# State products of heads 2 and 3 put on the other half of the array and into a second PSUM bank, and a new list of attention's order

## The chip, the cores and the metric

The kernel runs on one core of a Trainium2 chip. The metric is device time of one execution in microseconds (us). A core has five engines with a program each: TensorE (PE, with its weight loads shown apart as PEld), VectorE (DVE), ScalarE (ACT), GpSimd (POOL) and SyncE (SP, which here only issues DMAs). Each runs its own instructions in the order in which they were written and waits on semaphores for the others.

## The reference

```python
def _attn_ref(q, k, v, a_re, a_im):            # (4, 8, 768, 48) each
    mag = np.sqrt(a_re * a_re + a_im * a_im)
    scale = np.minimum(mag, 0.999) / (mag + 1e-06)
    a_re_n, a_im_n = (a_re * scale, a_im * scale)
...
    for t in range(S):                          # complex state, 48 x 48 a head
        new_re = ar * S_re - ai * S_im
        new_im = ar * S_im + ai * S_re
        S_re, S_im = (new_re + kv, new_im)
        y[:, :, t] = np.einsum('bhd,bhde->bhe', q[:, :, t], S_re)
...
def _moe_ref(x, w_gate, w1, w2):                # x: (3072, 384), 8 experts, F = 1024
    expert_idx = np.argmax(logits, axis=1)      # each token to one expert
...
        h = np.maximum(xe @ w1[e], 0.0)
        out[mask] = gate_w[mask, None] * (h @ w2[e])
```

## The kernel before

Attention comes first, then the experts. Attention is written in chunks of 128 positions: 4 batches of 6 chunks, 24 in all (chunk 2.3 is the fourth of the third batch). Ten *units* of one, two or three chunks (`UNITS`) go through `front`, elementwise work of ACT and DVE (logarithms, exponentials, scans and sines of the gates). Its last two DVE operations write `cz` and then `Z` of the unit, queries and keys turned by the accumulated phase, real and imaginary part; four small DMAs move the pieces of heads 6 and 7 to `cm`. Units 0 to 9 start at chunks 0.0, 0.1, 0.3, 1.0, 1.3, 2.0, 2.3, 3.0, 3.3 and 3.5.

`chunk` is PE's part. Per chunk there are transposes of the keys (L381, L383), scores into banks 0 and 1 (L394, and L402 for heads 6 and 7), which DVE masks into `am` (two operations), the **state products**, queries times the state that the earlier chunks left (L416, and L422 for heads 6 and 7; 20 chunks have them, a batch's first has none), `am` times values (L432), and, where more chunks follow, the new state (L442, L447). State products and value products accumulate in bank 4 (`YT`). ACT copies it to `yt` (L435), PE turns it (L455, bank 6, `XT`), ACT copies that to `xg` (L458). A float32 matmul shows as two MATMUL records. Heads lie in pairs: an even head on partitions 0 to 47, an odd one on 64 to 111, of the operands and of the result alike, `side(h)`:

```python
for g in range(G):                       # L416: three pairs of heads
    for part in range(2):
        for h in (2 * g, 2 * g + 1):
            nc.tensor.matmul(YT[side(h), g * 128:g * 128 + 128], lhsT=sb[1 - par][side(h), s0:s0 + D], rhs=wide[part][side(h), g, 0], ...)
```

After each batch (in pieces for the last) `route` takes the gate's argmax on DVE, counts places with small matmuls (L496 to L501) and POOL scatters rows to DRAM. When the last chunk is done, `fill` runs 256 tokens of the fullest expert (L616, L624), and then the eight experts follow (L784, L800), PE-bound, in an order that `M` plans by itself.

No engine is scheduled at run time: attention's operations are numbered as the code lists them, and `ORDER`, a list of these numbers in base 36, says in which order they are written. It sets the order on every engine and on SP's DMA queue. The duration that stands first in each `P.add` served the making of such a list; with the list given it does nothing. The first column of bank 7 holds ones (`ones_t`), which DVE's phase scans (L326) read.

Of the kernel before, what the change touches and what calls it, by code (L numbers as in the profile page):

```python
# [14 lines left out]
ACT = mybir.ActivationFunctionType  # L15
# [7 lines left out]
G = 3  # L23
# [5 lines left out]
SWAPPED = (2, 3, 7)  # L29
NZ = 4  # L30
# [26 lines left out]
0 1 1g 3 2 4 5 6 7 8 3e 9 1i 1j a c j b 1k 1h d e 1l l m k f n g 1m 3g i 3h h o 1n 1o p q r  # L57
1y 3i 1p 1r 3j s 1s t 3f 3k 1z 21 v 1q w 1u u 20 22 1t 10 3l 1v 1x 1w 6a 16 y 23 24 25 x 13 3m 3w 3n 3z 3p 27 26
3y z 3o 6c 3q 6d 14 28 3r 11 6e 15 17 3s 12 3x 3t 3u 29 2a 2b 2e 6f 40 6g 19 1c 41 6s 42 18 1a 43 6b 2c 44 2h 1d 2d 1b
3v 8r 45 2i 2j 6h 46 2k 2f 1e 49 6i 47 48 2g 2z 6j 6m 2w 30 8t 6k 6l 4a 2l 2n 2s 8u 2x 4b 31 2m bq 2y 6n 2t 1f 2o 4g 4d  # L60
6o 2p 6p 8v 4h 8w 4e 8x 3a 32 6t 2q 2r 6q 4i 6u bs 33 36 6r 35 6v 34 8y 2u 4j 4k 3b 6w 4f 6x 2v 6y 37 8z 4c 4m 4l 90 bt
6z 8s 38 39 71 4r 4v 4y br bu 51 52 4n 70 91 4o 53 3c 54 93 92 72 78 99 4p 4w 4s 4q 4z 55 5d 56 3d 95 73 bv 50 4x 5e 57
4t 94 74 98 bw 76 75 59 5g 7e 5f 9b 4u 58 77 9a 5b e5 7h bx 9c 7b 7c 5a 7f 96 5c 97 9d 7i by 7d 7g 5h bz 5i 7k 7j 5j 9e
7u c8 5k 9f 7r 7s 7v 7x c1 c0 c2 7y 9g 7t 7l 5l 7n 9h 80 7z 9j 9i e6 7w 8f 89 5m 7o 9k 5n 7m 5o 8g 81 8c c4 5p 7p 5v 8h
5w c3 e7 9p 9m 8a e8 c7 8i 5x 8d 82 5q 9l 83 85 7q 5r 5s 5t c9 9n 9o 8b 5y 5z 8e 9q 9t 9u 9r c5 h8 60 e9 ca c6 86 9s 9w
8n 84 9v cb ea a8 87 eb 9x 9y 5u ec 8j 8k 9z ha ab cd 8o cc 8l 68 65 ce ae 69 ed ee 8m eg 88 af 8p hb a0 ag ah a1 cf a4
# [927 lines left out]
```

## Time and profile before

| what | value |
|---|---|
| median of 3 runs | 494.07 us (489.94 to 500.96) |
| profiled execution | 494.87 us |
| its span, first to last instruction | 493.2 us |
| PE busy | 435.2 us (88%) |
| DVE busy | 245.2 us (50%) |
| ACT busy | 207.1 us (42%) |
| start of `fill`'s first matmul | 220.7 us |

The span is what the profile's rows cover; 1.7 us of the execution lie outside it. A start in the rows is counted from the span's start. Busy shares are means over attention and experts, which have different limits, so the stretches have to be read one by one.

### The profile page before, as it was taken

The page shows a single profiled execution, that of the slowest core. Times are in us where ns is not written, and L with a number is a line of the kernel's source. Part 1 is how long each engine was busy: PE and PEld are TensorE (multiplying, and loading weights), DVE is VectorE, ACT ScalarE, POOL GpSimd, SP SyncE. Part 2 cuts the span into 40 slices and gives each one's busy share as a digit, 9 for nine tenths or more (in the row PEclk, how much of TensorE's full clock was granted, in tenths as well). Part 3 has the DMA queues.
Part 4 walks back from the last instruction along what each step waited for, and adds up shares of the span by engine and source line. Part 5 has one row for each costly group of instructions (what it writes and reads, how often), then busy time and mean ns, then how long its engine had stood idle before and what let it go on. Part 6 is the DMA issues. An engine that isn't in the chain of part 4 may idle for free. (4 is left out here: it accounts for less than half of the span.)

```text
span 493.2 us, 10498 instructions
## 1 busy us (share of the span) xinstructions
PE 435.2 (88%) x4402; PEld 303.3 (62%) x4402; DVE 245.2 (50%) x436; ACT 207.1 (42%) x319; POOL 89.3 (18%) x156
## 2 busy tenths in 40 slices
PE   0134998989898889989999999999999999999995
PEld 0023887878787788977775545555555455655563
DVE  6999999999988877733321131312212012111101
ACT  5999999989979577722001001000000010000000
POOL 8100022053203817022100000100101020010102
PEclk9999999999989998999999999999999999999999
DMA  8347674655948444561999832912504313010001
GB/s 277 117 170 225 197 276 95 229 171 167 247 117 268 113 143 116 135 247 60 282 391 373 208 83 48 282 60 96 130 0 161 105 72 132 16 32 17 28 1 47
DMA packets 31542, 73.11 MB, mean 148 GB/s; under 512 B 19955, under 2 KB 21900, under 8 KB 28160
## 3 DMA queue, kind: packets, MB, share of 16 engines
q1 hardware_dynamic: 28160, 62.49, 42.0%
q0 software_dynamic: 3184, 9.86, 5.3%
q8 instruction: 36, 0.59, 0.5%
q14 instruction: 18, 0.15, 0.1%
q10 hardware_dynamic: 144, 0.03, 0.0%
HBM read 55.65 MB, written 12.29 MB: 138 GB/s over the span
## 5 line engine op out<-in xcount | busy, mean ns | idle before, releaser
L784 PE MATMUL bank<-xrt,w1b 128*128 128x432 f32 (+6 forms) x336 | 114.5, 498 | 0.0
L800 PE MATMUL bank<-w2b,ht 128*128 128x384 f32 x336 | 110.7, 486 | 0.0
L792 ACT ACTIVATE ht<-bank 128x384 f32<-128x384 f32 (+1 forms) x32 | 14.8, 464 | 223.1 <-PE bank L784 223.1
L784 PEld LDWEIGHTS bank<-xrt,w1b 128*128 128x128 f32 x336 | 63.7, 190 | 48.8 <-issue 22.9
L800 PEld LDWEIGHTS bank<-w2b,ht 128*128 128x128 f32 x336 | 63.8, 190 | 44.5 <-issue 1.4
L789 DVE TENSOR_SCALAR ht<-bank 128x384 f32<-128x384 f32 (+1 forms) x32 | 16.8, 524 | 92.0 <-PE bank L784 91.5
L632 POOL DMA_INDIRECT out_dram<-yo,hg x22 | 21.6, 980 | 220.7 <-DVE yo L724 175.0
L724 DVE TENSOR_SCALAR yo<-bank,hg 128x384 f32<-128x384 f32 x22 | 13.6, 618 | 83.6 <-PE bank L800 83.6
L259 ACT ACTIVATE AB<-AB 128x1152 f32<-128x1152 f32 (+5 forms) x46 | 45.5, 998 | 3.8 <-DVE first L572 1.6
L515 POOL DMA_INDIRECT xs_hbm<-xg,slot x24 | 33.4, 1391 | 39.1 <-issue 13.9
L159 POOL TENSOR_TENSOR Z<-Z,C 128x1152 f32<-128x1152 f32 (+2 forms) x7 | 16.0, 2288 | 126.0 <-DMA AB<-in_gates_u_dram 48.2
L381 PE MATMUL bank<-order,cz 128*128 128x128 f32 x60 | 11.4, 305 | 28.3 <-DVE cz L159 22.2
L159 DVE TENSOR_TENSOR am<-bank,mask 128x512 f32<-128x512 f32 x48 | 31.6, 681 | 7.3 <-PE bank L402 3.8
L159 DVE TENSOR_TENSOR Z<-Z,AB 128x1152 f32<-128x1152 f32 (+4 forms) x20 | 31.7, 1589 | 3.5 <-ACT AB L259 3.1
L432 PE MATMUL bank<-am,v 128*48 128x128 f32 x384 | 28.4, 291 | 5.6 <-DVE am L159 5.0
L394 PE MATMUL bank<-Z 48*64 48x64 f32 (+1 forms) x576 | 30.8, 255 | 2.4 <-DVE Z L159 1.2
L394 PE MATMUL bank<-cz 48*64 48x64 f32 (+1 forms) x576 | 29.9, 262 | 0.8 <-DVE am L159 0.4
L682 ACT ACT_TABLE_LOAD x23 | 29.5, 1283 | 1.7 <-PEq L979 1.3
L416 PE MATMUL bank<-cz,sb 48*48 48x128 f32 x240 | 24.9, 275 | 3.1 <-issue 2.0
L432 PEld LDWEIGHTS bank<-am,v 128*48 128x48 f32 x384 | 22.9, 131 | 7.1 <-DVE am L159 5.2
L416 PE MATMUL bank<-Z,sb 48*48 48x128 f32 x240 | 24.7, 270 | 2.4 <-issue 2.4
L394 PEld LDWEIGHTS bank<-Z 48*64 48x64 f32 x576 | 24.1, 141 | 3.2 <-issue 1.6
(166 smaller groups left out, 632.8 us busy)
## 6 DMA issues: line engine op xcount, KB each, us to landing
w2b<-in_w_dram SPq DMA_DIRECT2D x7, 1536.0 KB
w1b<-in_w_dram SPq DMA_DIRECT2D x7, 1536.0 KB
AB<-in_gates_u_dram SPq DMA_DIRECT2D x6, 1152.0 KB
Z<-in_qk_u_dram SPq DMA_DIRECT2D x6, 1152.0 KB
v<-in_v_u_dram SPq DMA_DIRECT2D x8, 792.0 KB
wA<-in_w_dram SPq DMA_DIRECT2D x4, 768.0 KB
xs_hbm<-htA SPq DMA_DIRECT2D x2, 1045.0 KB
xr<-xs_hbm SPq DMA_DIRECT2D x12, 156.0 KB
```

What stands on the lines that cost most here:

```text
L159: return (eng or nc.vector).tensor_tensor(out=o, in0=a, in1=b, op=op)
L259: lambda: nc.scalar.activation(o, i, func=f, scale=scale, bias=bias, **kw), r, w, tag)
L394: nc.tensor.matmul(SC[h % 2][y:y + 64, g * 128 + x:g * 128 + 128], lhsT=wide[part][side(h), g, 1, x:x + 64], rhs=wide[part][side(h), g, 0, ...
L416: nc.tensor.matmul(YT[side(h), g * 128:g * 128 + 128], lhsT=sb[1 - par][side(h), s0:s0 + D], rhs=wide[part][side(h), g, 0], start=(g == 0 ...
L432: nc.tensor.matmul(YT[side(h), (h // 2) * 128:(h // 2) * 128 + 128], lhsT=values(h), rhs=am[2 * par + h % 2][:, h // 2, :], start=(c == 0 ...
L515: i = nc.gpsimd.indirect_dma_start(out=xs_hbm[:, :], out_offset=bass.IndirectOffsetOnAxis(ap=R[slot][:, c:c + 1], axis=0), in_=xg[:, (g0 + ...
L632: i = nc.gpsimd.indirect_dma_start(out=out[:, :], out_offset=bass.IndirectOffsetOnAxis(ap=index, axis=0), in_=y, in_offset=None, bounds_ch ...
L682: nc.scalar.preload_act_table_set("natural_log_exp_and_others" if P.cur == "LE" else "trig_and_small")
L784: nc.tensor.matmul(HB[hb][:, 0:nt], lhsT=a[:, c:c + 128], rhs=xrt[s][:, d, 0:nt], start=(d == 0), stop=(d == DT - 1))
L789: M.add("DVE", 0.00105 * n + 0.12, lambda o=o, k=k, n=n, hb=hb: nc.vector.tensor_scalar_max(o, HB[hb][:, k:k + n], 0.0), (("H", hb),), (ko,))
L792: M.add("ACT", 0.00085 * n + 0.12, lambda o=o, k=k, n=n, hb=hb: nc.scalar.activation(o, HB[hb][:, k:k + n], func=ACT.Relu), (("H", hb),), ...
L800: nc.tensor.matmul(OB[ob][:, 0:DM], lhsT=ht[s][:, f_, j * 128 - k0:j * 128 - k0 + 128], rhs=w[:, f_ * DM:f_ * DM + DM], start=(f_ == 0), s ...
```

## The change

`PLACE` gives each pair of heads its 128 columns of `yt`: pair 0 stays at 0, pair 2 moves to 128, pair 3 to 256, pair 1 (heads 2 and 3) to 384. Heads 2 and 3 write to bank 7 (`YU`), with sides exchanged: head 2 (operands on partitions 0 to 47) to partitions 64 to 111, head 3 to 0 to 47. The loop of the state products has part outside and pairs inside. ACT copies 384 columns of bank 4 and 128 of bank 7, two instructions per chunk for one. The turning matrix and the gate's weights follow the exchanged sides. The ones move to column 511 of bank 7, bank 7 is set to zero at the start, and the scans no longer name bank 7 as an operand of the plan. The whole of `ORDER` is new. The planned duration of a state product goes from 1.345 to 0.95.

```diff
+PLACE = (0, 3, 1, 2)
...
-0 1 1g 3 2 4 5 6 7 8 3e 9 1i 1j a c j b 1k 1h d e 1l l m k f n g 1m 3g i 3h h o 1n 1o p q r
+0 1 1h 3h z 3 2 4 1i 5 6 3i 6h 7 1j 8 1k 9 1l 1m j a b c d k 1n l e f m 1o g 3j i h 3k o n p
...
-    ones_t = bank[7][:, 0:1]
-    nc.vector.memset(ones_t, 1.0)
-    for x in (4, 0, 1):
+    for x in (4, 0, 1, 7):
         nc.vector.memset(bank[x], 0.0)
     nc.vector.memset(bank[5], 0.0)
+    ones_t = bank[7][:, 511:512]
+    nc.vector.memset(ones_t, 1.0)
...
-                    (Bk, ("tend", b, c0), "b7"), (("si", s, g),))
+                    (Bk, ("tend", b, c0)), (("si", s, g),))
...
+            def out(h):
+                g = h // 2
+                o = 64 * (h % 2 != (g == 1))
+                x = 128 * PLACE[g]
+                return YU[o:o + D] if g == 1 else YT[o:o + D, x:x + 128]
...
-                    for g in range(G):
-                        for part in range(2):
+                    for part in range(2):
+                        for g in range(G):
                             for h in (2 * g, 2 * g + 1):
                                 s0 = part * G * D + g * D
-                                nc.tensor.matmul(YT[side(h), g * 128:g * 128 + 128], lhsT=sb[1 - par][side(h), s0:s0 + D],
-                                                 rhs=wide[part][side(h), g, 0], start=(g == 0 and part == 0), stop=False, skip_group_check=True)
-                P.add("PE", 1.345, f, (("sb", 1 - par),) + ZK[0] + ZK[1], (("YT", 0), ("YT", 1)))
+                                nc.tensor.matmul(out(h), lhsT=sb[1 - par][side(h), s0:s0 + D],
+                                                 rhs=wide[part][side(h), g, 0], start=(g < 2 and part == 0), stop=False, skip_group_check=True)
+                P.add("PE", 0.95, f, (("sb", 1 - par),) + ZK[0] + ZK[1], ("YT", "b7"))
...
-            P.add("ACT", act_t(512) - 0.06, lambda: nc.scalar.copy(yt[par], YT), (("YT", 0), ("YT", 1)), (("yt", par),))
+            P.add("ACT", act_t(384) - 0.06, lambda: nc.scalar.copy(yt[par][:, 0:384], YT), ("YT",), (("yt", par),))
+            P.add("ACT", act_t(128) - 0.06, lambda: nc.scalar.copy(yt[par][:, 384:512], YU), ("b7",), (("yu", par),))
...
-                        nc.tensor.matmul(XT[x:x + 64, p * 104:p * 104 + 104], lhsT=yt[par][:, p * 128 + x:p * 128 + x + 64], rhs=turn[:, p, :],
+                        nc.tensor.matmul(XT[x:x + 64, p * 104:p * 104 + 104], lhsT=yt[par][:, PLACE[p] * 128 + x:PLACE[p] * 128 + x + 64], rhs=turn[:, p, :],
```

**PE, the first state products (chunk 0.1).** `sb` is the state, `cz` and `Z` are the two parts, `cm` the pieces of heads 6 and 7, `bank4` and `bank7` the results; x2 is a pair of heads. Before:

```order
L383 MATMUL bank2_63<-order_95,cm1_204 128x112
L416 MATMUL bank4_65<-cz1_201,sb0_216 48x128 x2
L416 MATMUL bank4_65<-Z1_194,sb0_216 48x128 x2
L416 MATMUL bank4_65<-cz1_201,sb0_216 48x128 x2
L416 MATMUL bank4_65<-Z1_194,sb0_216 48x128 x2
L416 MATMUL bank4_65<-cz1_201,sb0_216 48x128 x2
L416 MATMUL bank4_65<-Z1_194,sb0_216 48x128 x2
L381 MATMUL bank3_64<-order_95,Z2_195 128x128 x3
```

And now:

```order
L424 MATMUL bank4_65<-cz1_202,sb0_217 48x128 x2
L424 MATMUL bank7_68<-cz1_202,sb0_217 48x128 x2
L424 MATMUL bank4_65<-cz1_202,sb0_217 48x128 x2
L424 MATMUL bank4_65<-Z1_195,sb0_217 48x128 x2
L424 MATMUL bank7_68<-Z1_195,sb0_217 48x128 x2
L424 MATMUL bank4_65<-Z1_195,sb0_217 48x128 x2
L464 MATMUL bank6_67<-turn_114,yt0_215 64x104 x8
```

The same twelve matmuls follow each other as three pairs of one part and then three of the other, the second pair of each in bank 7.

**DVE, the end of unit 5 (first chunk 2.0).** `cz2` and `Z1` are the unit's results, `am0` and `am1` the masked scores of chunk 1.4, `am2` and `am3` those of chunk 1.5; the rows with `lend` are scans of unit 6, `AB1<-AB1,C1` is a product of unit 7. Before:

```order
L313 TENSOR_SCALAR AB0_190<-AB0_190 128x1152
L315 SCALAR_TENSOR_TENSOR AB0_190<-AB0_190,lend_69,C0_197 128x384
L159 TENSOR_TENSOR am0_208<-bank0_61,mask_100 128x512
L159 TENSOR_TENSOR am1_209<-bank1_62,mask_100 128x512
L315 SCALAR_TENSOR_TENSOR AB0_190<-AB0_190,lend_69,C0_197 128x384 x2
L159 TENSOR_TENSOR AB1_191<-AB1_191,C1_198 128x1152
L159 TENSOR_TENSOR cz2_202<-Z1_194,AB2_192 128x2304
L159 TENSOR_TENSOR Z1_194<-Z1_194,AB2_192 128x2304
L291 COPY lend_69<-AB0_190 128x3x3
L159 TENSOR_TENSOR am3_211<-bank1_62,mask_100 128x512
L159 TENSOR_TENSOR am2_210<-bank0_61,mask_100 128x512
```

And now:

```order
L315 TENSOR_SCALAR AB0_191<-AB0_191 128x1152
L161 TENSOR_TENSOR am2_211<-bank0_61,mask_101 128x512
L317 SCALAR_TENSOR_TENSOR AB0_191<-AB0_191,lend_69,C0_198 128x384
L161 TENSOR_TENSOR cz2_203<-Z1_195,AB2_193 128x2304
L161 TENSOR_TENSOR am1_210<-bank1_62,mask_101 128x512
L161 TENSOR_TENSOR Z1_195<-Z1_195,AB2_193 128x2304
L161 TENSOR_TENSOR am0_209<-bank0_61,mask_101 128x512
L317 SCALAR_TENSOR_TENSOR AB0_191<-AB0_191,lend_69,C0_198 128x384 x2
L161 TENSOR_TENSOR AB1_192<-AB1_192,C1_199 128x1152
L328 SCALAR_TENSOR_TENSOR AB0_191<-bank7_68,tend_71,AB0_191 128x384
L161 TENSOR_TENSOR am2_211<-bank0_61,mask_101 128x512
L293 COPY lend_69<-AB0_191 128x3x3
```

(The first `am2` of the second list is chunk 1.3's.) Two scans, a product and one mask stood ahead of `Z1` and now stand behind it, but chunk 1.5's masks stand further back, with one phase scan more ahead of them.

**ACT, the copies of the first chunk's result (chunk 0.0).** `yt` receives bank 4, and now bank 7 too; rows with `AB` belong to units. Before:

```order
L259 ACTIVATE AB2_192<-AB2_192 128x1152
L259 ACTIVATE AB2_192<-AB2_192,hpi_81 128x1152
L450 COPY sb0_216<-bank5_66 112x384
L435 COPY yt0_214<-bank4_65 128x512
L259 ACTIVATE AB2_192<-AB2_192 128x1152
```

And now:

```order
L444 COPY yt0_215<-bank7_68 128x128
L261 ACTIVATE AB2_193<-AB2_193 128x1152
L459 COPY sb0_217<-bank5_66 112x384
L443 COPY yt0_215<-bank4_65 128x384
L261 ACTIVATE AB2_193<-AB2_193 128x1152
```

One copy became two, here with two other instructions between them.

## Rows read from the trace of the kernel before

**Rows 1.** The page's busy lines, its 40 slices of 12.3 us (tenths of busy time, the granted clock, the DMA share) and its lines on instruction packets.

```profile
PE 435.2 (88%) x4402; PEld 303.3 (62%) x4402; DVE 245.2 (50%) x436; ACT 207.1 (42%) x319; POOL 89.3 (18%) x156
PE   0134998989898889989999999999999999999995
DVE  6999999999988877733321131312212012111101
ACT  5999999989979577722001001000000010000000
q8 instruction: 36, 0.59, 0.5%
q14 instruction: 18, 0.15, 0.1%
```

**Rows 2.** Busy time by stretch: from, to and length in us, then PE, PEld, DVE, ACT, POOL with instruction counts, granted clock, DMA share, GB/s.

```profile
50.00:125.00 75.00, 71.03 (x1536) 61.10 (x1529) 74.17 (x85) 72.84 (x96) 16.46 (x10) 1.00 0.63 190
125.00:207.00 82.00, 72.95 (x1556) 64.39 (x1555) 65.81 (x117) 64.76 (x102) 28.82 (x20) 0.96 0.58 166
221.00:243.00 22.00, 22.00 (x101) 15.94 (x100) 8.06 (x47) 3.46 (x10) 4.13 (x5) 1.00 0.47 135
243.00:489.00 246.00, 244.76 (x818) 141.84 (x816) 45.35 (x99) 16.69 (x52) 23.74 (x25) 1.00 0.37 119
```

**Rows 3.** PE in order of time: start, us to the last end, operation and count. One chunk's state products and what follows.

```profile
120.47 0.42 PE L416 MATMUL bank<-cz,sb 48*48 48x128 f32 x4
120.72 0.39 PE L416 MATMUL bank<-Z,sb 48*48 48x128 f32 x4
120.94 0.39 PE L416 MATMUL bank<-cz,sb 48*48 48x128 f32 x4
...
121.91 0.43 PE L422 MATMUL bank<-cm,sb 112*48 112x128 f32 x4
122.17 1.05 PE L432 MATMUL bank<-am,v 128*48 128x128 f32 x16
123.04 0.88 PE L455 MATMUL bank<-turn,yt 128*64 128x104 f32 x16
```

**Rows 4.** The same view: three transposes on the whole array, and one chunk's scores (48 matmuls of 128 or 64 columns into two banks, from the first row of L394 to L402).

```profile
89.18 0.49 PE L381 MATMUL bank<-order,cz 128*128 128x128 f32 x3
89.51 0.36 PE L383 MATMUL bank<-order,cm 112*128 112x112 f32 x2
89.79 0.44 PE L394 MATMUL bank<-cz 48*64 48x128 f32 x8
...
91.05 0.56 PE L402 MATMUL bank<-cm 112*64 112x128 f32 x8
```

**Rows 5.** The state products alone, by stretch: PE, PEld (instructions), clock, DMA share, GB/s. 24 matmul records are a chunk.

```profile
48.00:125.00 77.00, 13.83 (x216) 11.38 (x216) 1.00 0.63 192
125.00:221.00 96.00, 17.95 (x264) 14.54 (x264) 0.96 0.60 175
148.50:221.00 72.50, 14.09 (x208) 11.16 (x204) 0.98 0.58 173
```

**Rows 6.** ACT's copies by line: count, busy us, mean ns, idle time before them and who ended it.

```profile
L385 ACT COPY kt<-bank 128x384 f32<-128x384 f32 x40 | 17.9, 479 | 1.1 <-PE bank L383 1.0
L435 ACT COPY yt<-bank 128x512 f32<-128x512 f32 x24 | 14.1, 588 | 9.5 <-PE bank L432 9.2
```

**Rows 7.** DVE in order of time around the end of unit 5.

```profile
115.03 1.26 DVE L159 TENSOR_TENSOR am<-bank,mask 128x512 f32<-128x512 f32 x2
116.21 1.92 DVE L315 TENSOR_TENSOR_SCAN AB<-AB,lend,C 128x384 f32<-128x384 f32 x2
118.04 1.33 DVE L159 TENSOR_TENSOR AB<-AB,C 128x1152 f32<-128x1152 f32 x1
119.29 2.55 DVE L159 TENSOR_TENSOR cz<-Z,AB 128x2304 f32<-128x2304 f32 x1
121.95 2.56 DVE L159 TENSOR_TENSOR Z<-Z,AB 128x2304 f32<-128x2304 f32 x1
124.50 1.28 DVE L159 TENSOR_TENSOR am<-bank,mask 128x512 f32<-128x512 f32 x2
125.70 1.01 DVE L326 TENSOR_TENSOR_SCAN AB<-bank,tend,AB 128x384 f32<-128x384 f32 x1
```

**Rows 8.** PE's first work on unit 5 (scores of chunk 2.0), and on unit 6 (scores of chunk 2.3), with the idle time before it.

```profile
125.84 0.44 PE L394 MATMUL bank<-cz 48*64 48x128 f32 x8 [0.39 <-DVE am L159]
148.94 0.32 PE L394 MATMUL bank<-cz 48*64 48x128 f32 x1
```

**Rows 9.** DVE between the ends of units 5 and 6: every row of that stretch with idle time before it, and unit 6's last product.

```profile
141.60 0.33 DVE L471 TENSOR_REDUCE lg<-xg 128x24 f32<-128x96 f32 x1 [0.79 <-ACT xg L458]
142.81 0.69 DVE L159 TENSOR_TENSOR am<-bank,mask 128x512 f32<-128x512 f32 x1 [0.89 <-PE bank L402]
143.42 2.55 DVE L159 TENSOR_TENSOR Z<-Z,AB 128x2304 f32<-128x2304 f32 x1
```

**Rows 10.** PE stopping with "issue" as the reason, in order of time, and a wait for the last batch's counts.

```profile
136.19 0.33 PE L447 MATMUL bank<-v,kt 128*48 128x48 f32 x3 [2.00 <-issue]
158.08 0.31 PE L416 MATMUL bank<-Z,sb 48*48 48x128 f32 x2 [2.12 <-issue]
184.22 0.20 PE L496 MATMUL bank<-oh,before 128*128 128x48 bf16 x1 [1.24 <-ACT C L259]
188.49 0.41 PE L394 MATMUL bank<-Z 48*64 48x128 f32 x3 [0.41 <-issue]
189.23 0.29 PE L394 MATMUL bank<-Z 48*64 48x128 f32 x2 [0.33 <-issue]
189.97 0.34 PE L394 MATMUL bank<-Z 48*64 48x64 f32 x3 [0.45 <-issue]
216.97 0.42 PE L416 MATMUL bank<-cz,sb 48*48 48x128 f32 x4 [1.31 <-issue]
```

**Rows 11.** The view of rows 2, of the first of these stops, of the 3.2 us behind it and of a later stretch.

```profile
133.90:136.30 2.40, 0.40 (x16) 0.28 (x10) 2.33 (x7) 2.38 (x3) 0.00 (x0) 1.00 0.99 352
136.40:139.60 3.20, 3.20 (x24) 2.45 (x22) 3.20 (x4) 2.23 (x4) 0.00 (x0) 0.50 0.57 234
190.90:194.30 3.40, 3.40 (x59) 3.40 (x56) 3.03 (x4) 0.92 (x2) 3.10 (x2) 0.50 0.53 120
```

More of the change, by code (lines that the diff above doesn't have):

```diff
@@ L62 @@
[L62 to L66, printed above, removed]
@@ L80 @@
+n9 nj na ng ot nk nb ou pk nc nh ni nl nn pi nm ov pj l2 po ow pl ox oy oz p5 pm p0 p6 pp p1 p7 pb p2 pc p8 p3 pn p4 pu
+p9 pd pa pe pq pv pf ps pr pg py ph pw q2 px pt pz q3 q0 q1
 """
@@ L241, in gateloop_then_moe @@
         P = Plan()
-        SC, KT, YT, ST, XT, RT = bank[0:2], bank[2:4], bank[4], bank[5], bank[6], bank[6][:, 416:416 + C * E]
+        SC, KT, YT, YU, ST, XT, RT = bank[0:2], bank[2:4], bank[4][:, 0:384], bank[7][:, 0:128], bank[5], bank[6], bank[6][:, 416:416 + C * E]
         def act_t(n):
@@ L411, in f @@
                 def f():
[L412 to L413 removed]
+                    for part in range(2):
+                        for g in range(G):
                             for h in (2 * g, 2 * g + 1):
                                 s0 = part * G * D + g * D
[L416 to L418 removed]
+                                nc.tensor.matmul(out(h), lhsT=sb[1 - par][side(h), s0:s0 + D],
+                                                 rhs=wide[part][side(h), g, 0], start=(g < 2 and part == 0), stop=False, skip_group_check=True)
+                P.add("PE", 0.95, f, (("sb", 1 - par),) + ZK[0] + ZK[1], ("YT", "b7"))
                 def f():
                     for j in range(2):
[L422 removed]
+                        nc.tensor.matmul(out(6 + j), lhsT=sb[1 - par][0:112, 2 * G * D + j * D:2 * G * D + j * D + D],
                                          rhs=last2[:, j, 0], start=False, stop=False, skip_group_check=True)
[L424 removed]
+                P.add("PE", 0.25, f, (("sb", 1 - par), "YT") + MK, ("YT",))
             def values(h):
@@ L431, in f @@
                 for h in range(H):
-                    nc.tensor.matmul(YT[side(h), (h // 2) * 128:(h // 2) * 128 + 128], lhsT=values(h),
-                                     rhs=am[2 * par + h % 2][:, h // 2, :], start=(c == 0 and h < 2), stop=True, skip_group_check=True)
-            P.add("PE", 0.88, f, (("v", i % NV), ("am", 2 * par), ("am", 2 * par + 1), ("YT", 0), ("YT", 1)), (("YT", 0), ("YT", 1)))
-            P.add("ACT", act_t(512) - 0.06, lambda: nc.scalar.copy(yt[par], YT), (("YT", 0), ("YT", 1)), (("yt", par),))
+                    nc.tensor.matmul(out(h), lhsT=values(h),
+                                     rhs=am[2 * par + h % 2][:, h // 2, :], start=(c == 0 and h < 4), stop=True, skip_group_check=True)
+            P.add("PE", 0.88, f, (("v", i % NV), ("am", 2 * par), ("am", 2 * par + 1), "YT", "b7"), ("YT", "b7"))
+            P.add("ACT", act_t(384) - 0.06, lambda: nc.scalar.copy(yt[par][:, 0:384], YT), ("YT",), (("yt", par),))
+            P.add("ACT", act_t(128) - 0.06, lambda: nc.scalar.copy(yt[par][:, 384:512], YU), ("b7",), (("yu", par),))
             if not last:
```

46 lines of the change are left out of this document (24 added, 22 removed).

## The prediction, made before the changed kernel ran

> **What bounds the kernel now.** I read the page's slices first. DVE stands at 9 from the second slice to the twelfth, ACT at 8 or 9 to the eleventh, PE at 8 or 9 from the fifth to the end [rows 1]. So attention has a part where three engines are full at once, and the experts are PE's alone. The view by stretches confirms it: from 50 to 125 us DVE is busy 74.17 of 75 us and ACT 72.84, PE 71.03; from 125 to 207 us PE has 72.95 of 82 us and DVE and ACT some 65 each; from 221 us on PE is busy all but 1.2 us [rows 2]. The first matmul of `fill` follows attention's last value products and nothing in the change touches what comes behind it, so I take the 22 us of `fill` and the 246 us of the experts as a block that moves as a whole. The question is by how much attention ends earlier than 221 us.
>
> Second, the waits. At 125.84 us PE begins the scores of chunk 2.0 after a wait for DVE, and DVE's `Z` of unit 5, which these scores also need, ended at 121.95 + 2.56 = 124.51 us [rows 7, 8]. So until 125 us DVE sets the pace, and what PE saves there is lost in waiting. Unit 6's `Z` ends at 143.42 + 2.55 = 145.97 us [rows 9] and PE takes it up at 148.94 us [rows 8]: from there PE is the late one. In both stretches PE also stops with "issue" as reason: 2.00, 2.12 and 1.31 us are the large ones [rows 10]. During the first, DVE and ACT went on, the DMA share was 0.99, and the clock granted afterwards was 0.50, its 1.2 GHz level, for 3.2 us or so [rows 11]. Instructions come by DMA as well (36 and 18 packets [rows 1]), so packets that wait behind bulk loads are the reading that I give "issue".
>
> **The state products.** Four records (two heads, two records each) of 128 columns start every 0.22 to 0.25 us [rows 3], 55 ns a record at the smaller, while three whole-array transposes of 128 columns take 89.51 - 89.18 = 0.33 us, 110 ns each [rows 4]. So two heads of a pair already run side by side, each at 110 ns, and a chunk costs 12 x 0.11 = 1.32 us. Scores use all four quarters of the array and two banks: 48 records in 91.05 - 89.79 = 1.26 us, 26 ns each [rows 4]. With heads 2 and 3 on the other two quarters and in another bank, pairs 0 and 1 can run together; pairs 0 and 2 share their quarters, so these remain: 2 pairs x 2 parts x 2 records x 0.11 = 0.88 us. That saves 0.44 us a chunk, 8.8 us over 20 chunks. From below the bound is 0 (two at a time stays the limit), from above 0.70 us (26 ns a record as in the scores, 1.32 - 24 x 0.026), though the shared quarters speak against that end. I take 0.44: the scores' row is the same shape of work. The value products keep 16 records, alternating less regularly between halves (left, right, right, left); their 0.87 us [rows 3] stays, at most 0.2 us a chunk more if two heads on one half follow each other badly.
>
> A rule speaks against it. The Trainium skill, TensorEngine Tiling (Array Packing), section Restrictions and Gotchas, says that different row tiles cannot access the same PSUM bank at the same time. The two heads of a pair are on different row tiles and write bank 4, and they overlap all the same [rows 3, 4], on different partitions; by the rule a chunk would take 24 x 0.11 = 2.6 us before. Here the trace disagrees; if the rule came back with four at a time, two would remain and nothing would be saved, which is the second rival below.
>
> **Until 125 us: -1 us.** Nine chunks' state products lie there (216 records [rows 5]); their 4.0 us are covered by DVE, which has 0.8 us free in 75 [rows 2]. ACT gets 24 copies more. 512 columns take 588 ns and 384 take 479 [rows 6], 0.85 ns a column, so 128 should take 479 - 256 x 0.85 = 261 ns and a chunk costs 479 + 261 - 588 = 0.15 us more. Some 10 of the 24 fall where ACT is full: 1.5 us, of which I count 1 as a loss, since ACT has 2.2 us free there. The added memset of bank 7 is one more of DVE's first instructions, when DVE waits for the first loads; it costs nothing, at most 0.5 us. On DVE the end of unit 5 moves forward past two scans, a product and a mask: (118.04 - 116.21) + (119.29 - 118.04) + (116.21 - 115.03)/2 = 3.7 us [rows 7]. But the scores of chunk 2.0 also need the score banks, which the masks of chunk 1.5 free, and those have one phase scan (0.95 us) more ahead of them. So I count nothing for it here.
>
> **From 125 to 149 us: +3 us.** PE's work shrinks by three state products, 1.3 us, and the stop of 2.00 us with the half clock behind it (3.2 us at half rate, 1.6 us of work lost [rows 10, 11]) may go or stay. DVE bounds it: up to unit 6's `Z` the lists hold the same work to within 0.2 us, and DVE idled 0.79 + 0.89 = 1.68 us between the two units' ends [rows 9], so `Z` can come 1.7 us earlier; with the 2.9 us that PE lags (148.94 - 145.97), PE can gain 4.6 us by the scores of chunk 2.3. Between 0 and 4.6 I take 3, nearer to the upper end, since the order now gives PE the masks when it needs them and three shorter products come on top.
>
> **From 149 us on: +3.5 us,** eight state products (208 records [rows 5]) x 0.44, on PE's own path: DVE had 16 us free from 125 to 207 [rows 2] and can follow.
>
> **Packets: +1.5 us.** Behind 149 us PE stopped 2.12 + 0.41 + 0.33 + 0.45 + 1.31 = 4.6 us for issue [rows 10]. The new list moves loads on SP past other work, so these stops move too; no row tells where to. Between -5 (as many again) and +4.6 I take a third of what stands there.
>
> Sum: -1 + 3 + 3.5 + 1.5 = 7.0 us. The profiled execution (494.87 us) is 0.8 us from the median of the runs, so I subtract from the median: 494.07 - 7.0 = **487.1 us**. A measurement of this kernel tells some 2%, 9.9 us, from no change.
>
> **The rivals.** *The stops go as well.* Then 125 to 149 us gives 4.6, the 4.6 us of stops vanish, and so do the half clock of 190.9 to 194.3 us (3.4 us at half rate, 1.7 us [rows 11]) and the 1.24 us wait at 184.22 us [rows 10]: -1 + 4.6 + 3.5 + 4.6 + 1.7 + 1.2 = 14.6, less a third for stops that arise elsewhere, 10 to 14: about 482. For it: DVE had 16 us free. Against: 54 packets must still come through the same loads. *Two at a time stays the limit,* or DVE's masks hold PE: 3.5 falls away, 3 becomes 1.5: -1 + 1.5 + 0 + 1.5 = 2, 492 us. *Slower:* PE now goes through its 24 instructions faster, and its packets fall more often into stretches with a DMA share near 1. Each such stop costs what the first one did, 2.0 us and 1.6 us at half clock, 3.6 us. It decides between 125 and 221 us: two more such stops eat the gain, five give 494.07 - 7 + 18 = 505 us.
>
> **How the numbers follow.** The forecast (484 to 490.5) has 0.47, the stops going 0.23, no gain 0.22, slower 0.08. The range reaches from 478 (the first rival with 15.6) to 497 (one stop more than no gain), which leaves out some 0.1 at the bottom of the first and 0.1 at the slower end. Faster by over 2% (below 484.2) is the first rival and a little of the forecast, 0.27; slower by over 2% (above 503.9) the far half of the last, 0.04; within 2%, 0.69.
>
> **What would show it.** State products of 24 records in 0.85 to 0.95 us; bank 4's copy at 0.48 us and bank 7's at 0.26; unit 5's `Z` near 121 us but chunk 2.0's scores near 125; chunk 2.3's scores near 146; `fill` beginning near 214 us and 272 us from there to the span's end, as now (493.2 - 220.7). I am wrong if the state products keep 55 ns a record, if `fill` begins at 221 us or later although they are short, or if the experts no longer follow without a gap.

## The result, and the profile after

The changed kernel takes 496.54 us (median of 20 runs, 493.69 to 498.75) against 492.5 us for the kernel before in its company (median of 20). The ratio is 1.0075, 95% interval 1.0053 to 1.0097: **slower by 0.75%, some 4 us**, where 7 us of gain were forecast. Ratios, here and below, leave out runs over 1.5% longer than the fastest of their kernel. The profiled execution took 494.33 us (span 492.6 us), one of the shorter of its runs, while that of the kernel before (494.87 us) was one of the longer of its own. So the two profiles differ by only -0.5 us and hide the loss; what each stage did can still be read from them.

Busy time by stretch, changed kernel, columns as in [rows 2]:

```profile
50.00:125.00 75.00, 64.80 (x1295) 52.77 (x1293) 71.25 (x81) 70.77 (x97) 16.11 (x9) 0.93 0.59 180
125.00:207.00 82.00, 73.46 (x1719) 62.10 (x1715) 67.78 (x120) 68.94 (x120) 23.76 (x22) 1.00 0.59 170
```

Until 125 us VectorE, which sets the pace there, does 71.25 us of work where it did 74.17: it stands idle for 3.75 us where it did for 0.83. From `fill` to the end of the span it takes 492.6 - 219.9 = 272.7 us, as before (272.5).

The parts that were forecast for themselves came out. One chunk's state products, PE in order of time (answers [rows 3]; here 24 records), and ACT's copies by line (answers [rows 6]):

```profile
110.40 0.53 PE L424 MATMUL bank<-cz,sb 48*48 48x128 f32 x10
110.67 0.31 PE L424 MATMUL bank<-Z,sb 48*48 48x128 f32 x2
110.77 0.28 PE L424 MATMUL bank<-cz,sb 48*48 48x128 f32 x2
110.82 0.66 PE L424 MATMUL bank<-Z,sb 48*48 48x128 f32 x10
```

```profile
L443 ACT COPY yt<-bank 128x384 f32<-128x384 f32 x24 | 11.6, 482 | 4.8 <-PE bank L440 4.7
L444 ACT COPY yt<-bank 128x128 f32<-128x128 f32 x24 | 6.4, 269 | 1.6 <-DVE AB L328 1.6
```

Four heads run side by side now, and from the first to the last start there are 0.81 us (median of the chunks) where there were 1.25. The copies take 0.48 and 0.27 us. But the second copy's line says something new: it waited 1.6 us for L328, a VectorE line that has no data for it. L328 are the phase scans, and their factor of ones stands in column 511 of bank 7, the bank into which heads 2 and 3 now go. The scans' group, first of the kernel before, then of the changed one (count, busy us, mean ns, idle us before them and who ended it):

```profile
L326 DVE TENSOR_TENSOR_SCAN AB<-bank,tend,AB 128x384 f32<-128x384 f32 (+2 forms) x30 | 24.7, 842 | 0.0
```

```profile
L328 DVE TENSOR_TENSOR_SCAN AB<-bank,tend,AB 128x384 f32<-128x384 f32 (+2 forms) x30 | 25.0, 847 | 6.4 <-PE bank L424 3.1 <-PE bank L440 1.2 <-ACT C L261 1.1
```

And the list of waits of the changed kernel (who waits, for whom: us in total, times, longest), five of the eight rows that pair L328 with the two lines and the copy that use bank 7:

```profile
DVE AB L328 <- PE bank L424: 3.1, 1, 3.1
PEld bank L424 <- DVE AB L328: 1.7, 2, 1.1
ACT yt L444 <- DVE AB L328: 1.6, 3, 0.6
DVE AB L328 <- PE bank L440: 1.2, 2, 0.9
DVE AB L328 <- ACT yt L444: 0.9, 4, 0.3
```

The two sides wait for each other. Around 101 us it goes back and forth; PE first, then VectorE, both in order of time:

```profile
100.96 0.42 PE L424 MATMUL bank<-cz,sb 48*48 48x128 f32 x4 [0.39 <-ACT yt L443]
102.18 0.44 PE L424 MATMUL bank<-cz,sb 48*48 48x128 f32 x8 [0.80 <-DVE AB L328]
103.58 1.05 PE L440 MATMUL bank<-am,v 128*48 128x128 f32 x16
```

```profile
101.11 1.02 DVE L328 TENSOR_TENSOR_SCAN AB<-bank,tend,AB 128x384 f32<-128x384 f32 x1 [0.20 <-ACT yt L444]
104.25 1.02 DVE L328 TENSOR_TENSOR_SCAN AB<-bank,tend,AB 128x384 f32<-128x384 f32 x1 [0.87 <-PE bank L440]
```

The scan at 101.11 us waits for the copy of chunk n - 1 out of bank 7; the state products of chunk n stop before their first write of that bank until the scan is over; and the next scan waits for the value products that go there.

Not all of the scans' 6.4 us count alike. The wait of 3.1 us is a single one that ended at 199.25 us, where VectorE no longer sets the pace. Between 50 and 125 us the scans stood idle 0.33 + 0.20 + 0.87 = 1.40 us for users of bank 7, of VectorE's 3.75.

**By stages.** VectorE's `Z` of unit 5, its masks of chunks 1.5 (two rows) and 2.2, with a stop between them, PE's first scores of chunks 2.0 and 2.3 (they answer [rows 8]), and the first matmul of `fill`, all of the changed kernel; then chunk 2.2's second mask and the first matmul of `fill` of the kernel before:

```profile
121.81 2.56 DVE L161 TENSOR_TENSOR Z<-Z,AB 128x2304 f32<-128x2304 f32 x1 [0.36 <-ACT AB L261]
130.44 0.67 DVE L161 TENSOR_TENSOR am<-bank,mask 128x512 f32<-128x512 f32 x1
131.10 0.68 DVE L161 TENSOR_TENSOR am<-bank,mask 128x512 f32<-128x512 f32 x1
144.32 2.56 DVE L161 TENSOR_TENSOR cz<-Z,AB 128x2304 f32<-128x2304 f32 x1 [1.32 <-issue]
152.11 1.26 DVE L161 TENSOR_TENSOR am<-bank,mask 128x512 f32<-128x512 f32 x2
132.81 0.44 PE L402 MATMUL bank<-cz 48*64 48x128 f32 x8
153.21 0.54 PE L402 MATMUL bank<-cz 48*64 48x128 f32 x5
219.89 0.89 PE L625 MATMUL bank<-AB,wA 128*128 128x256 f32 x3
```

```profile
145.89 0.68 DVE L159 TENSOR_TENSOR am<-bank,mask 128x512 f32<-128x512 f32 x1
220.72 0.68 PE L616 MATMUL bank<-AB,wA 128*128 128x256 f32 x2
```

Chunk 1.5's masks end at 131.78 us; before, at 124.50 + 1.28 = 125.78 us [rows 7]: 6.0 us late. From there to the end of chunk 2.2's masks it takes 153.37 - 131.78 = 21.6 us (before 146.57 - 125.78 = 20.8), and on to `fill` 219.89 - 153.37 = 66.5 us (before 220.72 - 146.57 = 74.2). So -6.0, -0.8 and +7.6 us: the last stage gains what the first one loses.

The prediction counted by PE's first scores. Chunk 2.0's come 132.81 - 125.84 = 7.0 us late; from there to chunk 2.3's it takes 20.40 us (before 23.10 [rows 8]), and on to `fill` 66.68 us (before 71.78): **-7.0, +2.7 and +5.1 us, where -1, +3 and +5 (with the packets) were forecast**. This profile is 2.2 us below its kernel's median; a later one of the same kernel, near its median (496.74 us, the first of the last three runs below), has these marks at 133.82, 153.77 and 222.27 us: -8.0, +3.2 and +3.3, the same shape.

PE's stops with "issue" as the reason from 149 to 221 us, from the list of waits, before and after (answers [rows 10]):

```profile
PE bank L416 <- issue: 3.9, 4, 2.1
PE bank L394 <- issue: 1.2, 3, 0.5
PE bank L432 <- issue: 0.6, 2, 0.3
PE bank L447 <- issue: 0.5, 1, 0.5
```

```profile
PE bank L424 <- issue: 1.6, 1, 1.6
PE bank L440 <- issue: 0.9, 4, 0.3
PE bank L464 <- issue: 0.6, 2, 0.3
PE bank L402 <- issue: 0.3, 1, 0.3
```

They went from 6.2 to 3.4 us. The half clock of [rows 11] has gone from 136 and 191 us; two stretches at 0.50, the 1.2 GHz level, stand earlier, at 67.1 and 74.0 us, each behind a stop of PE (2.2 and 1.7 us):

```profile
67.20:70.40 3.20, 3.20 (x60) 2.85 (x52) 3.16 (x4) 3.18 (x4) 0.00 (x0) 0.50 0.99 364
74.10:80.70 6.60, 6.40 (x107) 5.43 (x105) 6.45 (x6) 6.57 (x9) 0.00 (x0) 0.50 0.30 76
```

### The profile page after: what moved, and what is told of

Same layout as the page of the kernel before. It is cut to its first block, busy times and chain, and to the rows that moved or that the text cites. A ratio compares the mean times of both kernels' runs of the same rounds, so it can differ in the third digit from the quotient of the medians.

```text
span 492.6 us, 10524 instructions
## 1 busy us (share of the span) xinstructions
PE 434.3 (88%) x4402; PEld 296.0 (60%) x4402; DVE 244.2 (50%) x437; ACT 209.0 (42%) x343; POOL 83.3 (17%) x156
## 5 line engine op out<-in xcount | busy, mean ns | idle before, releaser
L402 PE MATMUL bank<-cz 48*64 48x64 f32 (+1 forms) x576 | 32.6, 273 | 26.4 <-DVE cz L161 22.4
L402 PEld LDWEIGHTS bank<-cz 48*64 48x64 f32 x576 | 24.4, 148 | 30.5 <-DVE cz L161 22.4
L524 POOL DMA_INDIRECT xs_hbm<-xg,slot x24 | 28.9, 1204 | 55.6 <-DVE slot L517 24.9
L402 PE MATMUL bank<-Z 48*64 48x128 f32 (+1 forms) x576 | 32.7, 267 | 1.0 <-DVE Z L161 0.7
L328 DVE TENSOR_TENSOR_SCAN AB<-bank,tend,AB 128x384 f32<-128x384 f32 (+2 forms) x30 | 25.0, 847 | 6.4 <-PE bank L424 3.1
L402 PEld LDWEIGHTS bank<-Z 48*64 48x64 f32 x576 | 24.9, 149 | 2.0 <-DVE Z L161 1.5
L464 PE MATMUL bank<-turn,yt 128*64 128x104 f32 x384 | 23.7, 266 | 1.6 <-ACT xg L467 0.9
```

The costliest lines, as they stand in the source:

```text
L328: P.add("DVE", T * 0.00209 + 0.11, lambda g=g: nc.vector.tensor_tensor_scan(im[:, g, :], bc(ones_t, [128, T]), im[:, g, :], tend[:, b, g, ...
L402: nc.tensor.matmul(SC[h % 2][y:y + 64, g * 128 + x:g * 128 + 128], lhsT=wide[part][side(h), g, 1, x:x + 64], rhs=wide[part][side(h), g, 0, ...
L464: nc.tensor.matmul(XT[x:x + 64, p * 104:p * 104 + 104], lhsT=yt[par][:, PLACE[p] * 128 + x:PLACE[p] * 128 + x + 64], rhs=turn[:, p, :], st ...
L524: i = nc.gpsimd.indirect_dma_start(out=xs_hbm[:, :], out_offset=bass.IndirectOffsetOnAxis(ap=R[slot][:, c:c + 1], axis=0), in_=xg[:, (g0 + ...
```

## The experiments

Theory A: the mutual waits through the ones' bank ate the gain. Theory B: the new list costs by itself. C, D, E, F and G arose on the way. The median of the kernel before was 484 to 498 us in the five comparisons, so each kernel is put beside runs of it from its own comparison, and where a size matters three kernels ran in one. The chip alone does not explain the spread: chip 15 had 484.4 us beside the first four runs and 498.0 beside the first with spread ones.

**Ones out of the bank, and the two lists apart.**

```diff
-    ones_t = bank[7][:, 511:512]
-    nc.vector.memset(ones_t, 1.0)
+    ones_t = one
```

> The changed kernel, with one edit: the phase scans take their factor of ones from the constant `one` in SBUF instead of column 511 of bank 7. In the profile of the changed kernel these scans stood idle 6.4 us for PE and ACT, and PE and ACT some 2.1 and 3.0 us for them, none of which the kernel before has. Theory A (the ones' column in bank 7 makes scans, products and copies wait for each other, and that eats the gain): these waits fall below 1 us together, and the time comes out at 487 to 490 us, 0.988 to 0.996 of the kernel before. Theory B (the new list itself costs: PE is idle longer between 50 and 75 us and falls to half clock twice early on): the waits vanish, others take their place, and the time stays at 1.003 to 1.010 of the kernel before.

> The changed kernel's code with the order of the kernel before: each copy of bank 7 stands right behind its copy of bank 4, and two first matmuls of `fill` have changed places. Ones stay in bank 7. Theory A: the old list did not reckon with waits between scans and bank 7 either, so they cost here as well, and the time is 1.004 to 1.015 of the kernel before. Theory B: the shorter state products bring their gain under the old list: 0.988 to 0.996.

> Both edits: the changed kernel's code, the order of the kernel before, and the ones in SBUF. Theory A: the shorter state products show, 0.988 to 0.996 of the kernel before, and some 1 to 2% below the same code with the ones in bank 7. Theory B: the same as with the ones in bank 7, within 0.3%. If neither holds and it stays at 1.000, the state products' 0.44 us a chunk are hidden under other waits whatever the list.

> The kernel before with the new list alone (the 24 copies of bank 7 left out of it): state products two at a time into bank 4, nothing of attention in bank 7 but the ones. Theory A: the new list by itself is harmless, 0.996 to 1.004 of the kernel before. Theory B: the new list is what costs, and without the shorter products it costs more: 1.010 to 1.020.

Ratios to the kernel before, with 95% intervals: changed kernel with `one` 1.0067 (1.0024 to 1.0109); its code under the old list 1.0228 (1.0172 to 1.0284), the same with `one` 1.0149 (1.0100 to 1.0197); old code under the new list 1.0102 (1.0047 to 1.0157). The last speaks for B. Under the old list A's ranges were missed, with the ones in bank 7 (1.004 to 1.015 expected) and with `one` (a gain expected). The first looks like a refutation of A, until one reads the scans' group of that run, and two of its scans in order of time, with what POOL does then:

```profile
L328 DVE TENSOR_TENSOR_SCAN AB<-one,tend,AB 128x384 f32<-128x384 f32 (+2 forms) x30 | 33.4, 1129 | 0.0
```

```profile
63.41 4.25 DVE L328 TENSOR_TENSOR_SCAN AB<-one,tend,AB 128x384 f32<-128x384 f32 x2
63.63 3.21 POOL L161 TENSOR_TENSOR Z<-Z,C 128x1152 f32<-128x1152 f32 x1 [50.29 <-DVE AB L312]
```

The waits are gone (0.0), but the scans cost 8.4 us more: the two take 4.25 us where with the bank's column they took 1.93, for the second does not end before POOL's product has. Five of the 30 scans meet a product in this way and take 2.1 to 3.4 us; the others keep the time that they had. The Trainium skill, SBUF — State Buffer, section Who interferes with whom, says that a VectorE instruction with two SBUF inputs contends with a GpSimd instruction that reads SBUF, and that the order of issue decides who blocks. The trace agrees: POOL's product began during the first scan and took 3.21 us where it took 2.63 in the changed kernel, and the second scan ended 0.8 us after the product. So this edit swapped one wait for another, and its ratio says nothing for or against A.

**The two prices, each alone in the kernel before.** The first kernel reads `one` there; the second keeps its ones in PSUM, but in bank 6, which `turn` products write:

```diff
-    ones_t = bank[7][:, 0:1]
+    ones_t = bank[6][:, 511:512]
```

> The kernel before, with one edit: the phase scans take their ones, broadcast, from the constant `one` in SBUF. Where that edit was made in the changed kernel, the 30 scans took 1129 ns each where they take 847 from the bank, 8.4 us of VectorE more. Theory A (the ones' place matters on both sides: waits if it is bank 7, slower scans if it is that constant): the scans take 1.1 us here too, VectorE sets the pace until 125 us, and the time is 1.008 to 1.018 of the kernel before. Theory C (what costs in the changed kernel are the second copy and the turned sides, wherever the ones stand): 0.997 to 1.004 here, since neither is in this kernel.

> The kernel before, with its ones in column 511 of bank 6, which the turning products write and the copies of `xg` read, and not in bank 7, which attention leaves alone there. Code, list and all else as before: the suspected cost by itself. Theory A: scans, turns and copies now wait for each other, some 6 us of waiting on VectorE as in the changed kernel, and the time is 1.008 to 1.022 of the kernel before. Theory C: such waits are absorbed, 0.998 to 1.004.

1.0108 (1.0056 to 1.0160) with `one`, the scans at 1061 ns: as A said, and against C. 1.0239 (1.0181 to 1.0297) with bank 6, rather more than A said: 12 us for a column of ones in a bank that others use, all else being equal. Its list of waits has both directions again, and a third party, the batch's counts (L496), which share the bank:

```profile
PE bank L496 <- DVE AB L326: 5.4, 2, 3.6
DVE AB L326 <- PE bank L455: 4.2, 3, 1.9
DVE AB L326 <- ACT xg L458: 2.8, 3, 1.9
```

**A full row of ones in SBUF,** on the thought that the broadcast of one column made the scans slow:

```diff
+    ones_t = const([128, TU], "ones_t", 1.0)
...
-                    im[:, g, :], bc(ones_t, [128, T]), im[:, g, :], tend[:, b, g, c0:c0 + 1], ALU.mult, ALU.add),
+                    im[:, g, :], ones_t[:, 0:T], im[:, g, :], tend[:, b, g, c0:c0 + 1], ALU.mult, ALU.add),
```

> The changed kernel with ones that stand in SBUF at full width, 384 columns a partition, so that no scan reads a bank and none reads one column over and over. If the slowness of the scans from `one` came from the broadcast, they take some 845 ns like the decay scans, which read two full operands from SBUF. Theory A: neither waits nor slower scans are left, and the time is 0.985 to 0.997 of the kernel before. Theory B (the new list costs by itself; with the old code it did, 1.0102): what the list costs stays and the shorter products pay it back, 0.998 to 1.006. Theory C: as the changed kernel was, 1.005 to 1.010.

> The changed kernel's code, the order of the kernel before, and the full-width ones in SBUF. Under that order the code took 1.0228 with the ones in bank 7 and 1.0149 with the constant `one`. Theory A: 0.985 to 0.997, the shorter state products at last without a price. Theory B: the same, and below the same code under the new list. Theory C: 1.008 or more, for the second copy and the sides remain.

1.0147 (1.0055 to 1.0239; from two of its six runs) and 1.0103 (1.0056 to 1.0150). The thought was wrong: the scans take 1148 and 1065 ns, and again those beside a POOL product are the long ones. These two say nothing for or against A.

**Ones in PSUM, but out of the way.** A column in each of banks 2 to 7, and a table by unit and head group that picks one not in use:

```diff
+ONES = ("333", "333", "333", "333", "232", "375", "573", "773", "353", "333")
...
-    ones_t = bank[7][:, 511:512]
-    nc.vector.memset(ones_t, 1.0)
+    for x in (2, 3, 4, 5, 6, 7):
+        nc.vector.memset(bank[x][:, 511:512], 1.0)
...
-                    im[:, g, :], bc(ones_t, [128, T]), im[:, g, :], tend[:, b, g, c0:c0 + 1], ALU.mult, ALU.add),
+                    im[:, g, :], bc(bank[int(ONES[u][g])][:, 511:512], [128, T]), im[:, g, :], tend[:, b, g, c0:c0 + 1], ALU.mult, ALU.add),
```

> The changed kernel with a column of ones in each of banks 2 to 7, and a small table (unit, head group) that says which one a phase scan reads: one in which neither a product nor a copy is under way when the list comes to that scan. So the scans keep their PSUM operand (1.01 us for 384 columns, free of the port that POOL's `Z` products hold, which made single scans from SBUF 2.1 to 3.4 us long) and hardly wait. Code and list else as in the changed kernel. Theory A (the mutual waits through the ones' bank ate the gain): scans idle under 1.5 us where it was 6.4, and the time is 0.988 to 0.998 of the kernel before. Theory B (the new list costs by itself, 1.0102 with the old code): 1.000 to 1.007.

> The changed kernel's code under the order of the kernel before, with the ones spread over banks 2 to 7 by a table of its own. With all ones in bank 7 this was 1.0228. Theory A: 0.985 to 0.997 of the kernel before, the shorter state products without the waits; Theory B: the same, and at least 0.3% below the same code under the new list. If it is 1.003 or more, the second copy and the further waits that it brings cost what the products save.

> As the changed kernel with spread ones, but the state products' loops are turned back: head groups outside, the two parts inside, so that the products of one pair follow each other and two run at a time. State products go from 0.88 back to some 1.3 us a chunk. If those 0.44 us lie on PE's path from 125 us on, as predicted, 3 to 4 us more than with the loops as changed (0.6 to 0.8%); if they are covered by waits, the same within 0.3%.

0.9916 (0.9867 to 0.9964), 1.0049 (0.9998 to 1.0101) and 0.9916 (0.9870 to 0.9963). Under the new list A's time came out, though its scans still stood idle for 4.2 us and not under 1.5. Under the old one the waits seem to cost as much (1.0228 against 1.0049, from two comparisons), but no gain is left, so A's range was missed there, and B's forecast, that the old list would be the better one for this code, fell too. The third run priced nothing, for its state products stayed at 0.81 us. One chunk of rows shows why; first this run, loops turned back, then a run with heads 2 and 3 on their old sides (the last one below):

```profile
109.97 0.45 PE L425 MATMUL bank<-cz,sb 48*48 48x128 f32 x8
110.22 0.41 PE L425 MATMUL bank<-Z,sb 48*48 48x128 f32 x8
110.44 0.39 PE L425 MATMUL bank<-cz,sb 48*48 48x128 f32 x4
110.66 0.39 PE L425 MATMUL bank<-Z,sb 48*48 48x128 f32 x4
```

```profile
110.47 0.86 PE L425 MATMUL bank<-cz,sb 48*48 48x128 f32 x12
111.16 0.82 PE L425 MATMUL bank<-Z,sb 48*48 48x128 f32 x12
```

Eight records, two pairs, take 0.25 us whichever loop is outside; it is the turned sides that let two pairs overlap. Without them twelve records take 0.69 us.

**What the short products and the early part of the new list are worth.** In the first and the third of these kernels heads 2 and 3 stay on their old sides (in `turn` and in the packed weights as well); the second has the first 300 entries of the old list and then the rest in the new order; the fourth is the smallest mending, one digit:

```diff
-                o = 64 * (h % 2 != (g == 1))
+                o = 64 * (h % 2)
```

```diff
-    ones_t = bank[7][:, 511:512]
+    ones_t = bank[3][:, 511:512]
```

> As the changed kernel with spread ones (0.9916), but heads 2 and 3 stay on their old sides: they still write bank 7, have their own copy, and the list is the same. Pairs 0 and 1 then share their quarters of the array, so the state products go back to two heads at a time, 1.25 us from first to last start instead of 0.81. This prices the 0.44 us by themselves (turning the loops back did not, for the products kept 0.81 us). Theory D (the new list lives on the short products): the 20 x 0.44 = 8.8 us come back in most part, 1.002 to 1.012 of the kernel before, as with the old code under the new list (1.0102). Theory E (the products are covered, the gain is the new list's or the second bank's): 0.989 to 0.995.

> The changed kernel's code with spread ones, and a list of two halves: the first 300 entries of the kernel before's order (to about the end of unit 4's phase work, some 95 us), then what is left in the new order. In the changed kernel PE has 18.4 us of work between 50 and 75 us, where it had 24.65 before, and falls to half clock twice by 81 us. Theory F (this early part of the new list is what the new list costs): PE is busy over 23 us there, the half clock moves or goes, and the time is 0.980 to 0.988 of the kernel before, below the whole new list's 0.9916. Theory G (VectorE sets the pace there and PE's gap is its slack): 0.989 to 0.996.

> The old order with the changed code, spread ones (1.0049), and heads 2 and 3 on their old sides: state products two at a time again under the old list. What is then left of the change is the second bank and the second copy. Theory D: the short products were worth something under this list too, so it comes out above 1.0049, at 1.008 to 1.020; theory E: 1.000 to 1.007, and then what stands above 1.000 is the second copy's price (24 x 0.15 us on ACT, and a turn that waits for both).

> The changed kernel with one edit: the column of ones stands in bank 3, which the transposes of one part write (0.4 us a chunk) and one copy of `kt` reads, and not in bank 7, which state and value products hold for most of a chunk. Theory A: most of the mutual waits go with this alone: 0.990 to 0.999 of the kernel before. If it needs the table, 1.002 to 1.008.

All on one chip: 1.0035 (1.0007 to 1.0064), 0.9953 (0.9925 to 0.9981), 1.0102 (1.0051 to 1.0152) and 0.9975 (0.9945 to 1.0004). So D's ranges came out and E's did not: the short products count. The second bank with its second copy, and what waits are left, costs about 1% under the old list (third); under the new one it costs nothing that shows, for new list, second bank and long products (first) are no slower than the new list with the old code (1.0102, in another comparison). The one digit turns the loss into no difference (0.9975). The half lists are the fastest version, 0.5% below the kernel before. PE's gap is indeed closed there; the stretch 50 to 75 us, changed kernel and half lists:

```profile
50.00:75.00 25.00, 18.38 (x318) 14.68 (x315) 24.56 (x26) 24.21 (x31) 2.63 (x1) 0.91 0.71 229
```

```profile
50.00:75.00 25.00, 22.43 (x509) 18.77 (x501) 24.73 (x29) 24.69 (x33) 2.64 (x1) 1.00 0.70 234
```

But 0.9953 is short of what F said, and 482.4 us against the 483.3 of the new list with the ones in bank 3 is 0.9 us. This lies in G's range: the gap was mostly slack beside VectorE. The early half clock moved with it, to 98.8 to 105.7 us; what it costs by itself no run shows.

**The sizes, on one chip.**

> The changed kernel as it is, beside its two relatives below on one chip, since the ratios so far come from several chips, on which the kernel before itself took from 484 to 498 us. Both theories: slower than the kernel before, 1.004 to 1.012.

> The changed kernel with spread ones, again, on the chip of the two beside it. Theory A with the size that it had across chips: 1.2 to 1.8% below the changed kernel, 6 to 9 us. If the chip made part of that: 0.5 to 1.2%, 2.5 to 6 us.

> Spread ones and heads 2 and 3 on their old sides, again, on the chip of the two above. Theory D: 0.44 us of each chunk that lies on TensorE's own path, 8 chunks or 3.5 us (0.7%), above the version with turned sides; if every chunk counted, 8.8 us (1.8%). Theory E: within 0.2% of it.

496.88, 493.38 and 496.13 us; the kernel before 492.79 us (491.42 by the runs that enter the ratios); ratios 1.0102 (1.0064 to 1.0140), 1.0029 (0.9990 to 1.0069), 1.0092 (1.0054 to 1.0131). So the waits cost 3.5 us here (resampling the runs gives 2.3 to 4.4, 95%), not the 8 that ratios from different comparisons suggested, and the short products are worth 2.75 us (1.6 to 3.7). The scans' groups of the first two show what the table removed, and that it did not remove all:

```profile
L328 DVE TENSOR_TENSOR_SCAN AB<-bank,tend,AB 128x384 f32<-128x384 f32 (+2 forms) x30 | 25.0, 848 | 8.9 <-PE bank L424 4.4 <-PE bank L440 3.6 <-ACT yt L444 0.9
```

```profile
L329 DVE TENSOR_TENSOR_SCAN AB<-bank,tend,AB 128x384 f32<-128x384 f32 (+2 forms) x30 | 24.9, 845 | 5.0 <-PE bank L573 3.2 <-ACT yt L445 1.3 <-ACT kt L394 0.3
```

From 50 to 125 us VectorE is busy 71.06 us in the first and 73.29 in the second: 2.2 of the 3.5 us come back there. And up to the masks of chunk 1.5 the scans wait 5.1 us for users of bank 7 in the first, 0.3 us for users of their banks in the second; these masks end at 132.79 and 128.14 us, 4.65 us apart. The longest of these waits, in the first:

```profile
130.52 1.02 DVE L328 TENSOR_TENSOR_SCAN AB<-bank,tend,AB 128x384 f32<-128x384 f32 x1 [2.19 <-PE bank L424]
```

## Why the prediction was wrong

**The missing term.** The sum had no place for the scans. The diff shows that they lost their entry "b7" in the plan, and that the ones moved to the end of a bank which PE now writes; I costed the memset and went on. The entry orders the list alone; the built program still keeps engines apart by bank, whatever the column, and the wait that it inserts binds VectorE, the engine that sets the pace, to PE and ACT. This is the step that failed: "Until 125 us: -1 us", with its sentence that VectorE's end of unit 5 moves forward by 3.7 us. It measured -7.0. `Z` of unit 5 ended at 124.37 us, not near 121. Chunk 2.0's scores came at 132.8, not 125. On one chip the waits made 2.7 us of such a delay at `Z` (124.64 us with the ones in bank 7, 121.95 with spread ones) and 4.65 at chunk 1.5's masks, which hold the scores up; the rest is the list's, below. I had read the end of unit 5 off the order of instructions, and not asked whether any of them had a new partner to wait for. The Trainium skill, PSUM — Partial Sum Buffer, section PSUM bank collisions raise a hardware error, says that two of the three engines may not be in the same bank on the same partitions at once, even at other addresses. The waits between columns 0 to 127 and column 511 agree with it; whether the chip would have erred without them was not tried. The prediction weighed another rule on banks, which changed nothing, and passed this one by. Measured: 3.5 us of the whole time on one chip, and 12 us for the kernel before with its ones in bank 6.

**From 125 to 149 us: +3 us** came out as +2.7 between PE's marks, but not for the reason given. It rested on VectorE's idle 1.68 us being free to take; VectorE gained nothing (-0.8), for the stop of 1.32 us ("issue") before unit 6's `cz` product, in the rows by stages above, took most of its place. What went from this stretch are PE's stop of 2.00 us and the half clock behind it; that these are the 2.7 us is not shown by a run. Chunk 2.3's scores came at 153.2, not 146, for the 7.0 us before them were not made up.

**From 149 us on: +3.5, packets: +1.5.** Together 5.1 us between PE's marks, 5.0 forecast, and in part by luck. The stops went from 6.2 to 3.4 us (2.8) and the half clock at 191 us went (1.7 by the prediction's own count), which leaves 0.6 us for the eight chunks' 3.5, probably because PE had work to make up here (below; not shown). The products' worth by itself, 2.75 us on one chip, agrees with that term; it was right in mechanism and near in size. The stops go with the occasion more than with the list: in the profiles of the two comparisons in which the kernel before took 484 us, PE's stops for issue before `fill` sum to 0 to 1.3 us (one 3.4), in the others to 3.3 to 9.1. With the list unchanged and the ones in bank 3, in one of the former, PE had none from 125 us on. The value products of one chunk there, and in the changed kernel the same products torn by short stops:

```profile
161.91 1.05 PE L440 MATMUL bank<-am,v 128*48 128x128 f32 x16
```

```profile
165.94 0.49 PE L440 MATMUL bank<-am,v 128*48 128x128 f32 x5 [0.26 <-issue]
166.72 0.52 PE L440 MATMUL bank<-am,v 128*48 128x128 f32 x5 [0.28 <-issue]
```

**The list.** The prediction took the new order for a gain or nothing. Under the old code it is a loss of 1.0%. On the one chip, by the ratios, list, second bank and second copy (with what waits the table leaves) cost 0.92% or 4.5 us, the short products give back 0.63%, the waits cost 0.73%: together 1.02%, 5.0 us. Each term is the step from one of these kernels to the next, so that they add up proves nothing; but the first is the largest, and the waits alone do not make the loss. Where within the list it lies stays open: the masks of chunk 1.5 are late by 2.3 to 3.4 us without the waits in bank 7 as well (they end at 128.1 and 129.2 us with spread ones, 128.9 with the old code, 128.3 with the half lists), so the early gap is not all of it. One trace of it shows in the rows by stretch: between 50 and 125 us PE gets through 1536 matmul records before, 1295 in the changed kernel and 1341 in the old code under the new list. Some 55 of those that are missing were done before 50 us; the others fall into the stage where PE is the late one. What that costs was not measured by itself.

**The rivals.** The state products did run four at a time, so "two at a time stays the limit" fell, though its 492 us is nearer to the result than the forecast. "Slower" had the right sign by the wrong mechanism: the issue stops shrank. The time lies in the range, 0.5 us from its upper end; by that end's own words, one stop (3.6 us) more than no gain (492), it would stand at 495.7, and the time outside.

## What to carry over

Before work moves into another PSUM bank, list everyone who touches that bank, readers of constants too: one column that one engine reads made it wait here for products and copies in other columns of the bank, and them for it. If that engine sets the pace, the price (3.5 us here) can be as large as the saving that the move was made for (2.75). And price a new order of work apart from the change that it comes with: under the old code this one alone cost 1.0%. A cheap operand in PSUM may be there for a reason; moving it to SBUF met POOL's products instead, and only another bank, chosen by when it is idle, was cheap.

## What was not expected of the hardware

- A VectorE scan with two SBUF operands is as fast as one with a PSUM operand (1.0 us for 384 columns) until a POOL product of SBUF operands runs beside it; then it takes up to 3.4 us, as long as that product.
- The order of the loops over the state products did not matter (0.81 us both ways); their quarters of the array did (1.25 us with the second bank but the old sides). Turned sides without a second bank were not tried.
- The kernel before had a median of 484 us in two of the comparisons, with a granted clock mostly of 0.99 to 1.00, and of 492.5 to 498 us in the others, mostly of 0.98 to 0.99. What makes the difference is not shown; it is not the chip alone (15 had both), and the stops for issue go with it. Differences of 1% were only to be read within one comparison: spread ones gave 0.9916 against the kernel before in one and 1.0029 in another.
